# Keep-warm products of an opening on TensorE: from one f32 product each to sets of single-pass products on full rows and on row halves (mLSTM scan and gated feed-forward, one Trainium2 core)

## The chip, the cores and the metric

One Trainium2 chip (trn2), one core. The metric is the device time of one execution in microseconds (us). Three runs of the kernel before took 532.8, 534.25 and 534.55 us; the median is 534.25.

## The reference, cut to what matters

Four batches, eight heads, 768 steps, heads of 40. Per step and head a 40x40 state is faded, gets an outer product, and is read by the query; then a feed-forward with two gates follows on all 3072 rows of 320.

```
m_new = max(f_gate + m, i_gate)
C = exp(f_gate + m - m_new) * C + exp(i_gate - m_new) * outer(v, k)
n = exp(f_gate + m - m_new) * n + exp(i_gate - m_new) * k
y = sigmoid(o_gate) * (C @ q) / max(|n . q|, 1)
x = y as rows of 320
out = (sigmoid(x @ w_gate) * (x @ w_val)) @ w_out
```

## The kernel before

The 768 steps are six chunks of 128, so there are 24 units (chunk, batch). Within a chunk the scan is done with matrices: transposes of q and k (tile `pt`), scores (`s`) against a decay matrix `d`, a product with v (`av`), an outer product that carries the state on (`cs`), and a transpose of the finished rows (`xt`) into the feed-forward's input. That input is split into a high part `xh` (copied by ScalarE, `dx`, L789) and a low part `xl` (VectorE, `dy`, L796). The weights are read as pairs of words, decoded on ScalarE and VectorE (tile `dc`, from the staging tiles `st`, `st2`, `st_o`) and split into high and low parts in the same way. The feed-forward up (`pg`, L865) and down (`po`, L903) then run as single-pass products of such parts, three where one f32 product would be.

The order of all work is written out by hand: every step puts a function under a short key, and the string ORDER names the keys in the order in which they are issued; each engine runs its instructions in that order. Buffers and their waits come from tile pools by tag; a tag with one buffer makes its next user wait for the last reader or writer of the one before.

The change lies in `opening()` (L928). `warm` is an f32 tile of zeros, 128x256, set by VectorE (key `iw`, L931). `warming()` (key `im`) multiplies it six times while the first inputs arrive. `keep_warm(n)` (L967, key `iq`, twelve of them) is one f32 product of 128x128 with 128 columns on `warm`, into the PSUM tag `pg1`; nothing reads it. An f32 product is shown by the trace as two records. In ORDER the twelve `iq` stand where TensorE waits for the two first units: `iq` 0 behind the last score of unit 1, `iq` 1 behind the product with v of unit 1, `iq` 2 to 5 behind `cs` of unit 1 and ahead of the transpose `d1` (its tile is `xt_1`), `iq` 6 and 7 behind `d1`, then the first `pg` product of the feed-forward (`t0`), then `iq` 8 to 11, then the rest of `t0`.

The tiles that these steps meet: the tag `pg1` is also the second half of the first feed-forward pair; the tag `po1` holds a score of unit 1 and later a feed-forward result; the tag `gl` holds the low part of the gated values, two buffers, first used by VectorE about 33 us into the span.

Of the kernel before, what the change touches and what calls it, by code (L numbers as in the profile page):

```python
# [9 lines left out]
F32 = mybir.dt.float32  # L10
F32R = mybir.dt.float32r
# [223 lines left out]
def mlstm_then_gated_ffn_kernel(  # L235
# [13 lines left out]
    nc = tc.nc  # L249
    B, H, S, D = q.shape  # L250
    P = 128
    L = P
# [18 lines left out]
    two = ctx.enter_context(tc.tile_pool(name="two", bufs=2))  # L271
    dram = ctx.enter_context(tc.tile_pool(name="dram", bufs=1, space=bass.MemoryType.DRAM))
    ps_o = ctx.enter_context(tc.tile_pool(name="ps_o", bufs=1, space=bass.MemoryType.PSUM))
# [27 lines left out]
    def put(key, f, *args):  # L301
        todo.setdefault(key, []).append((f, args))
# [543 lines left out]
    gh, gl, po = {}, {}, {}  # L846
# [81 lines left out]
    def opening():  # L928
        us = ((0, 0), (0, 1))
        warm = two.tile([P, 2 * P], F32, tag="gh", name="warm")  # L930
        put("iw", nc.vector.memset, warm, 0.0)  # L931
        put("if", nc.sync.dma_start, fg, f_gate.rearrange("b h s -> (b h) s"))
        put("ii", nc.scalar.dma_start, ig, i_gate.rearrange("b h s -> (b h) s"))
        put("ie", nc.scalar.activation, warm[:1, P : P + 1], warm[:1, P : P + 1], AF.Exp)
# [31 lines left out]

        def keep_warm(n):  # L967
            pw = ps_o.tile([P, NT], F32, tag="pg1", name=f"pkeep{n}x")
            nc.tensor.matmul(pw[:, :P], warm[:, :P], warm[:, :P], start=True, stop=True)

        for n in range(PARAM["keep"]):
            put("iq", keep_warm, n)
# [92 lines left out]
    for c in range(NCH):  # L1065
        kc = PARAM["K"][c]
        tiles += [(c, j, 0, 2) for j in range(kc)] + [(c, j, 2, 4) for j in range(kc)]
        tiles += [(c, j, 0, 4) for j in range(kc, NF)]
    NU = NCH * B
    opening()  # L1070
    for n in range(len(tiles)):
        ffn_up(n)
# [25 lines left out]
    with tc.manual_schedule():  # L1098
        for word in ORDER.split():
# [3 lines left out]
            key, _, n = word.partition("*")  # L1103
            for _ in range(int(n or 1)):
                f, args = todo[key].pop(0)
# [30 lines left out]
```

## Time and profile before

| | |
|---|---|
| median of three runs | 534.25 us (532.8 to 534.55) |
| span of the profiled execution (its own time from the first to the last instruction) | 530.6 us |
| what the median has over that span | 3.65 us |
| TensorE busy | 518.2 us, 98% of the span, 4763 records |
| VectorE, ScalarE, GpSimd busy | 313.5, 218.8, 148.5 us |
| granted TensorE clock | 1.00 in all 40 slices |

A time in the trace counts from the span's start. Busy time of TensorE is the union of its products' records; a record's length holds the way through the array too, so products that follow closely overlap in it, and what one costs its successor is read from start to start. The share of 98% is a mean over the span: the stretch that the change touches, 16 to 25 us, and the one behind it, up to 50 us, are read apart. "Idle before <-releaser" is the time that an engine sat idle ahead of an instruction, and what ended it.

### The profile page before, as it was taken

How to read it: one execution, taken by the hardware profiler on the slowest of the kernel's cores; microseconds unless marked ns; L12 is line 12 of the kernel's file. 1: busy time of each engine (PE TensorE's matmuls, PEld its weight loads, DVE VectorE, ACT ScalarE, POOL GpSimd, SP SyncE). 2: the span in 40 equal slices, each digit the busy share in tenths (PEclk: the TensorE clock that was granted, in tenths of full speed). 3: DMA queues.
4: the chain of work that ended last, by engine and by line, in shares of the span. 5: the costliest groups of instructions: out<-in, count | busy, mean ns of one | idle time of the engine just before them, and what ended most of it. 6: DMA issues, size and time to landing. Idle time of an engine off the chain costs nothing.

```text
span 530.6 us, 12275 instructions
## 1 busy us (share of the span) xinstructions
PE 518.2 (98%) x4763; PEld 466.9 (88%) x4763; DVE 313.5 (59%) x783; ACT 218.8 (41%) x585; POOL 148.5 (28%) x219
## 2 busy tenths in 40 slices
PE   8969999999999999999999999999999999999997
PEld 6657988888999999998888888888888888999997
DVE  6999989887566557445645525646644553533323
ACT  6597676643524541443333443251333432212221
POOL 6544223455322312413124140334201101111110
PEclk9999999999999999999999999999999999999999
DMA  9998885423767965587388377578386364000000
GB/s 209 241 265 228 217 188 148 134 41 80 187 145 190 176 161 107 126 190 157 102 188 177 104 201 177 115 175 170 93 179 157 90 138 102 26 13 14 26 2 25
DMA packets 131649, 72.42 MB, mean 136 GB/s; under 512 B 103112, under 2 KB 120776, under 8 KB 131592
## 3 DMA queue, kind: packets, MB, share of 16 engines
q1 hardware_dynamic: 130504, 71.39, 56.9%
q8 instruction: 37, 0.61, 0.5%
q10 hardware_dynamic: 1088, 0.26, 0.3%
q14 instruction: 20, 0.16, 0.1%
HBM read 56.95 MB, written 14.68 MB: 135 GB/s over the span
## 4 chain that ended last, share of the span: by engine, by line
PE 88%; DVE 3%; DMA 3%; ACT 3%; issue 1%; POOL 1%; SPq 0%; DVEq 0%; ACTq 0%; POOLq 0%
PE pg L865 50%; PE po L903 23%; PE av L663 3%; PE pt L572 2%; PE s L693 2%; PE in L714 2%; PE cs L818 2%; DMA st_o<-in_moe_w_out_dram 2%; PE xt L783 1%; PE s L688 1%; ACT d L420 1%; DMA k<-in_k_dram 1%; DMA mscr<-m 1%; ACT dc L465 0%; ACT qk L587 0%
## 5 line engine op out<-in xcount | busy, mean ns | idle before, releaser
L878 ACT ACTIVATE sg<-pg 128x256 f32<-128x256 f32 (+1 forms) x103 | 48.4, 469 | 185.1 <-PE pg L865 174.9
L865 PE MATMUL pg<-xh,wh 128*128 128x256 f32 (+1 forms) x412 | 111.0, 337 | 2.6 <-ACT sg L878 2.5
L881 DVE SCALAR_TENSOR_TENSOR sg<-sg,pg 128x256 f32<-128x256 f32 (+1 forms) x103 | 54.1, 525 | 99.0 <-ACT sg L878 80.2
L865 PE MATMUL pg<-xl,wh 128*128 128x256 f32 (+1 forms) x412 | 109.7, 333 | 0.0
L865 PE MATMUL pg<-xh,wl 128*128 128x256 f32 (+1 forms) x412 | 108.9, 331 | 0.0
L892 POOL TENSOR_TENSOR gl<-sg,gh 128x256 fp32r<-128x256 f32 (+1 forms) x45 | 44.5, 988 | 186.0 <-ACT gh L886 107.1
L903 PE MATMUL po<-ol,gh 128*128 128x320 f32 x288 | 91.8, 321 | 0.0
L903 PE MATMUL po<-oh,gh 128*128 128x320 f32 x288 | 90.1, 318 | 0.9 <-ACT gh L886 0.9
L903 PE MATMUL po<-oh,gl 128*128 128x320 f32 x288 | 89.8, 318 | 0.0
L865 PEld LDWEIGHTS pg<-xh,wh 128*128 128x128 f32 x412 | 70.0, 188 | 8.6 <-ACT sg L878 4.0
L865 PEld LDWEIGHTS pg<-xl,wh 128*128 128x128 f32 x412 | 69.3, 188 | 5.3
L865 PEld LDWEIGHTS pg<-xh,wl 128*128 128x128 f32 x412 | 69.7, 188 | 4.6
L865 PE MATMUL pg<-xl,w 128*128 128x256 f32 (+1 forms) x206 | 59.3, 332 | 0.0
L903 PEld LDWEIGHTS po<-oh,gh 128*128 128x128 f32 x288 | 53.9, 188 | 4.3 <-ACT gh L886 1.4
L903 PEld LDWEIGHTS po<-oh,gl 128*128 128x128 f32 x288 | 54.0, 189 | 2.9 <-DVE gl L892 0.2
L903 PEld LDWEIGHTS po<-ol,gh 128*128 128x128 f32 x288 | 54.2, 189 | 2.2
L865 PE MATMUL pg<-xh,w 128*128 128x256 f32 (+1 forms) x206 | 53.5, 330 | 0.0
L699 DVE TENSOR_TENSOR d<-s,d 128x384 f32<-128x384 f32 (+1 forms) x66 | 33.2, 509 | 25.4 <-PE s L693 22.9
L420 ACT ACTIVATE d<-d,at 128x128 f32<-128x128 f32 x136 | 42.9, 392 | 2.8 <-DMA d<-mscr 2.8
L886 ACT ACTIVATE gh<-sg 128x256 fp32r<-128x256 f32 (+1 forms) x61 | 31.2, 512 | 28.7 <-DVE sg L881 24.5
L441 POOL TENSOR_SCALAR_AFFINE_SELECT d<-d 128x1024 f32<-128x1024 f32 x22 | 25.4, 1153 | 46.2 <-ACT d L420 28.4
L865 PEld LDWEIGHTS pg<-xl,w 128*128 128x128 f32 x206 | 36.1, 189 | 2.1
(168 smaller groups left out, 758.7 us busy)
## 6 DMA issues: line engine op xcount, KB each, us to landing
d<-mscr SPq DMA_DIRECT2D x22, 512.0 KB
ks<-scr SPq DMA_DIRECT2D x16, 360.0 KB
qs<-scr SPq DMA_DIRECT2D x16, 360.0 KB
k<-in_k_dram SPq DMA_DIRECT2D x24, 160.0 KB
v<-in_v_dram SPq DMA_DIRECT2D x24, 160.0 KB
o<-in_o_gate_dram SPq DMA_DIRECT2D x24, 160.0 KB
st_o<-in_moe_w_out_dram SPq DMA_DIRECT2D x12, 320.0 KB
out_dram<-ob SPq DMA_DIRECT2D x24, 160.0 KB
```

The costliest lines, as they stand in the source:

```text
L420: nc.scalar.activation(d[:, h, :], d[:, h, :], AF.Exp, bias=at[:, c, b * H + h : b * H + h + 1], scale=-1.0)
L441: nc.gpsimd.affine_select(out=d, in_=d, pattern=[[0, H], [1, L]], compare_op=ALU.is_ge, fill=0.0, base=0, channel_multiplier=-1)
L572: nc.tensor.transpose(pt[g][:r, x, :], t[u][:, h0 : h0 + nh, :].rearrange("p h d -> p (h d)"), ident)
L663: nc.tensor.matmul(dst[xs], lhs[:, xs], rhs, start=True, stop=True)
L693: nc.tensor.matmul(ps[g][:, m, :], ks[: 3 * D, 3 * m + g, :], qs[: 3 * D, 3 * m + g, :], start=True, stop=True)
L699: nc.vector.tensor_tensor(x, ps[g][:, :nh, :], x, ALU.mult)
L865: nc.tensor.matmul(pg[x], w[:, a, fs] if a < 2 else w[:, fs], y[c][:, a, n0:n1], start=first, stop=a == 2 and y is xl)
L878: nc.scalar.activation(sg[0], pg[0], AF.Tanh, scale=0.5)
L881: nc.vector.scalar_tensor_tensor(sg[0], sg[0], 1.0, pg[1], ALU.add, ALU.mult)
L886: nc.scalar.activation(gh[u][:, :nt], sg[0], AF.Copy)
L892: E('gl0' if c == 0 else 'gl', f'tl{n}').tensor_tensor(gl[u][:, :nt], sg[0], gh[u][:, :nt].bitcast(F32), ALU.subtract)
L903: nc.tensor.matmul(po[t], g[c, j, t0][:, (t - t0) * P : (t - t0 + 1) * P], o[:, j, :], start=j == 0 and first, stop=j == NF - 1 and last)
```

## The change

The twelve keep-warm steps stay where they are in ORDER, and the first set (`warming`) stays as it is. VectorE copies `warm` once into `zeros`, a tile of the single-pass type in the tag `gl`. Each `keep_warm(n)` becomes one of four sets of products with 256 columns on `zeros`, by n modulo 4: 0 is four pairs of half products (rows 0 to 63 into the tag `pg1`, rows 64 to 127 into the tag `po1`, in turn), 1 is four products on full rows, 2 is three times a full product and a pair of halves, 3 is four halves of the one kind and then four of the other. That is 8, 4, 9 and 8 products, three times each: 87 in place of 12.

```diff
         warm = two.tile([P, 2 * P], F32, tag="gh", name="warm")
-        put("iw", nc.vector.memset, warm, 0.0)
+        zeros = two.tile([P, 2 * P], F32R, tag="gl", name="zeros")
+
+        def blank():
+            nc.vector.memset(warm, 0.0)
+            nc.vector.tensor_copy(zeros, warm)
+
+        put("iw", blank)
...
         def keep_warm(n):
             pw = ps_o.tile([P, NT], F32, tag="pg1", name=f"pkeep{n}x")
-            nc.tensor.matmul(pw[:, :P], warm[:, :P], warm[:, :P], start=True, stop=True)
+            form = n % 4
+            pws = (pw, pw) if form == 1 else (pw, ps_o.tile([P, 4 * L], F32, tag="po1", name=f"pkeep{n}y"))
+            half = (slice(0, 64), slice(64, P))
+
+            def halves(y):
+                nc.tensor.matmul(pws[y][:, : 2 * P], zeros[half[y], :P], zeros[half[y]], start=True, stop=True)
+
+            def full():
+                nc.tensor.matmul(pws[0][:, : 2 * P], zeros[:, :P], zeros, start=True, stop=True)
+
+            if form == 0:
+                for x in range(4):
+                    halves(0)
+                    halves(1)
+            elif form == 1:
+                for x in range(4):
+                    full()
+            elif form == 2:
+                for x in range(3):
+                    full()
+                    halves(0)
+                    halves(1)
+            else:
+                for y in range(2):
+                    for x in range(4):
+                        halves(y)
```

On TensorE, between `cs` of unit 1 and the transpose of unit 1 (`xt_1`), the kernel before has the steps 2 to 5 as four products, each waiting for the one before it:

```order
L818 MATMUL cs_1_402<-v_1_234,k_1_136 80x82
L969 MATMUL pkeep2x<-warm 128x128 [waits PE_49]
L969 MATMUL pkeep3x<-warm 128x128 [waits PE_49]
L969 MATMUL pkeep4x<-warm 128x128 [waits PE_49]
L969 MATMUL pkeep5x<-warm 128x128 [waits PE_49]
L783 MATMUL xt_1_438<-ident,x_1_409 128x128 [waits DVE_49]
```

In the changed kernel 29 products stand there; from the ninth, the end of step 2, on (L980 is a half product, L983 a full one, x writes the tag `pg1` and y the tag `po1`):

```order
L980 MATMUL pkeep2y<-zeros 128x256
L980 MATMUL pkeep3x<-zeros 128x256 [waits PE_49]
L980 MATMUL pkeep3x<-zeros 128x256 x3
L980 MATMUL pkeep3y<-zeros 128x256 [waits PE_49]
L980 MATMUL pkeep3y<-zeros 128x256 x3
L980 MATMUL pkeep4x<-zeros 128x256 [waits PE_49]
L980 MATMUL pkeep4y<-zeros 128x256 [waits PE_49]
...
L983 MATMUL pkeep5x<-zeros 128x256 [waits PE_49]
L983 MATMUL pkeep5x<-zeros 128x256 x3
L783 MATMUL xt_1_479<-ident,x_1_422 128x128 [waits DVE_49]
```

The transpose stands behind 29 products in place of 4, with a wait of TensorE for itself at the start of each tile, x and y apart.

The same on TensorE between the first and the second product of the feed-forward (`pg_0_0_0`), steps 8 to 11, before:

```order
L865 MATMUL pg_0_0_0_472<-xh_407,wh_98 128x256 [waits Activation_49]
L969 MATMUL pkeep8x<-warm 128x128 [waits PE_49]
L969 MATMUL pkeep9x<-warm 128x128 [waits PE_49]
L969 MATMUL pkeep10x<-warm 128x128 [waits PE_49]
L969 MATMUL pkeep11x<-warm 128x128 [waits PE_49]
L865 MATMUL pg_0_0_0_472<-xh_407,wh_98 128x256
```

And in the changed kernel, its beginning and its end:

```order
L865 MATMUL pg_0_0_0_530<-xh_420,wh_98 128x256 [waits Activation_49]
L980 MATMUL pkeep8x<-zeros 128x256 [waits PE_49]
L980 MATMUL pkeep8y<-zeros 128x256 [waits PE_49]
...
L980 MATMUL pkeep11x<-zeros 128x256 [waits PE_49]
L980 MATMUL pkeep11x<-zeros 128x256 x3
L980 MATMUL pkeep11y<-zeros 128x256 [waits PE_49]
L980 MATMUL pkeep11y<-zeros 128x256 x3
L865 MATMUL pg_0_0_0_530<-xh_420,wh_98 128x256
```

Nothing else changes its place on any engine. VectorE has one row more, the copy into `zeros`, second in its queue.

## Rows read from the trace of the kernel before

**Rows 1.** The page, part 1: busy time of the engine, share of the span, records.
```profile
PE 518.2 (98%) x4763; PEld 466.9 (88%) x4763; DVE 313.5 (59%) x783; ACT 218.8 (41%) x585; POOL 148.5 (28%) x219
```

**Rows 2.** By stretch: busy us (records) of PE, PEld, DVE, ACT, POOL; PEclk; DMA share; GB/s.
```profile
25.00:30.00 5.00, 3.33 (x26) 2.89 (x25) 4.93 (x17) 4.57 (x15) 0.66 (x1) 1.00 1.05 281
30.00:35.00 5.00, 3.75 (x24) 2.68 (x22) 4.96 (x11) 5.00 (x19) 3.24 (x4) 1.00 0.79 223
35.00:40.00 5.00, 3.72 (x21) 2.75 (x22) 4.54 (x12) 4.23 (x13) 2.60 (x3) 1.00 1.00 279
40.00:50.00 10.00, 8.92 (x173) 7.04 (x172) 9.54 (x29) 7.77 (x23) 5.30 (x8) 1.00 0.80 200
...
60.00:120.00 60.00, 60.00 (x451) 50.97 (x449) 52.96 (x121) 36.96 (x94) 21.87 (x31) 1.00 0.56 136
```

**Rows 3.** The chain that ended last, 20 to 50 us: start us, us, what.
```profile
20.93 5.65 DMA st_o<-in_moe_w_out_dram
...
34.75 3.93 DMA st_o<-in_moe_w_out_dram
...
49.53 0.80 PE cs L818 x6
```

**Rows 4.** TensorE in order of time: start us, us, what, count, idle before.
```profile
16.27 0.39 PE L969 MATMUL pkeep0x<-warm 128*128 128x128 f32 x2
16.59 0.82 PE L663 MATMUL av<-v,d 128*32 128x41 f32 x64
17.33 0.49 PE L969 MATMUL pkeep1x<-warm 128*128 128x128 f32 x2
18.14 0.63 PE L783 MATMUL xt<-ident,x 128*128 128x128 f32 x3 [0.32 <-POOL x L761]
...
19.17 0.42 PE L969 MATMUL pkeep2x<-warm 128*128 128x128 f32 x2
19.65 0.49 PE L969 MATMUL pkeep3x<-warm 128*128 128x128 f32 x2
20.20 0.49 PE L969 MATMUL pkeep4x<-warm 128*128 128x128 f32 x2
...
21.23 0.55 PE L783 MATMUL xt<-ident,x 128*128 128x128 f32 x3
21.62 0.39 PE L969 MATMUL pkeep6x<-warm 128*128 128x128 f32 x2
...
22.36 0.38 PE L865 MATMUL pg<-xh,wh 128*128 128x256 f32 x1
...
24.49 0.37 PE L865 MATMUL pg<-xh,wh 128*128 128x256 f32 x1
...
25.63 0.64 PE L865 MATMUL pg<-xh,wl 128*128 128x256 f32 x4
...
26.35 0.28 PE L865 MATMUL pg<-xl,w 128*128 128x256 f32 x1
...
28.11 0.50 PE L865 MATMUL pg<-xh,wh 128*128 128x256 f32 x2 [1.31 <-ACT sg L878]
```

**Rows 5.** TensorE, the last products with v of unit 1, stretch 17.2 to 17.4.
```profile
17.00 0.40 PE L663 MATMUL av<-v,d 128*32 128x41 f32 x22
```

**Rows 6.** ScalarE in order of time.
```profile
21.82 0.49 ACT L789 ACTIVATE xh<-xt 128x384 fp32r<-128x384 f32 x1
...
27.69 0.37 ACT L878 ACTIVATE sg<-pg 128x256 f32<-128x256 f32 x1
...
36.38 0.44 ACT L465 ACTIVATE dc<-st 128x256 f32<-128x256 f32 x1 [0.37 <-DMA st<-in_moe_w_val_dram]
...
38.70 0.49 ACT L465 ACTIVATE dc<-st_o 128x320 f32<-128x320 f32 x1 [0.40 <-DMA st_o<-in_moe_w_out_dram]
```

**Rows 7.** VectorE in order of time.
```profile
0.93 0.27 DVE L1106 MEMSET warm<- 128x256 f32 x1 [0.93 <-PEq L1121]
3.31 0.41 DVE L1106 TENSOR_TENSOR_SCAN gin<-bmask,gin 32x128 f32<-32x128 f32 x1 [2.11 <-POOL ident masks.py:197]
```

## The prediction

> **What bounds the kernel now.** I read the busy time first, then the same by stretch, then the chain that ended last, then the order of time on TensorE and ScalarE. TensorE is busy 98% of the span [rows 1], but that is a mean. By stretch it idles between 25 and 50 us: 1.67, 1.25, 1.28 and 1.08 us are missing in the four stretches, 5.28 together, and from 60 to 120 us it has 60.00 of 60.00 [rows 2]. The chain agrees: at 20.93 us it runs through a weight transfer (`st_o`, 5.65 us to landing), then through ScalarE to a second one at 34.75 us, and only from 49.53 us on does it stay on TensorE [rows 3]. So TensorE is not what ends last in the opening, though its queue stands close behind; whatever lag it has when the stretch at 50 us begins stays to the end, since nothing idles there to take it up. The granted clock is 1.00 in every stretch read [rows 2], so the keep-warm products have no slow stretch left to repair, and I see nothing the change could win.
>
> **Prices.** Three are needed, all start to start, since records of neighbours overlap.
>
> A single-pass product with 256 columns: four of `pg` at 25.63 take 0.64 us, the last being about 0.28 long as the one at 26.35 [rows 4]; (0.64 - 0.28) / 3 = 0.12 us.
>
> A restart, where a new tile of a tag waits for the last product of the one before: the keep-warm tiles at 19.65 and 20.20 are 0.55 apart [rows 4]. Each holds one f32 product, two records of 128 columns and two passes each, as long in streaming as 256 single-pass columns, so about 0.11 each; 0.55 - 0.22 = 0.33 us per restart.
>
> A switch between full rows and halves, and whether two halves overlap, no row shows, since no product of this kernel lies on half the rows. The nearest rows are the products with v, which take a quarter of the columns: 64 records in 0.82 us [rows 4], 0.013 us each, while 41 columns in two passes at the price above need 0.12 x 82 / 256 = 0.04. So products on different quarters do overlap, and I take it that two halves of the rows do too: a pair costs 0.12, not 0.24. The other end is that they don't overlap. For the switch, the last record with v begins near 17.20 (17.00 + 0.40 less its length of some 0.2) [rows 5], and the full product behind it at 17.33 [rows 4]: about 0.12 us with next to nothing streamed between. I take 0.12 per switch; the ends are 0, if changing rows costs nothing, and 0.33, if it is a whole restart.
>
> **The change, step by step.** *The copy into `zeros`.* A copy of 128x256 on VectorE, about as long as the memset of that size, 0.27 us, stands ahead of an instruction that waits 2.11 us for GpSimd [rows 7]: nothing, and without that cover 0.27. The first set waits for the memset alone. The tag `gl` is used again by VectorE near 33 us, behind all keep-warm products: nothing.
>
> *Steps 0 and 1.* Four pairs in place of one f32 product: 0.48 for 0.21, and a switch. The products with v begin about 0.3 to 0.4 later than 16.59, step 1 near 17.7, and its four products end near 18.2. The transpose behind it waited for GpSimd until 18.14 [rows 4]. So it starts 0.1 late. The new wait of `pkeep0y` for VectorE's reading of the score is over by then. If the halves don't overlap, 0.5 more.
>
> *Steps 2 to 5.* With overlapping halves the four forms cost 6, 8, 4 and 4 prices of 0.12 (form 3 has four equal halves in a row, twice, so nothing to overlap with): 22 x 0.12 = 2.64. Three restarts (the y tile of step 4 waits for step 3, which ended just ahead of it) make 0.99, six switches inside form 2 make 0.72; the other switches fall into a restart. That is 4.35 us where 19.17 to 21.23 [rows 4] are 2.06: +2.29. The transpose `xt_1` starts near 23.6.
>
> *Steps 6 and 7.* They start 0.39 behind `xt_1` (21.23 to 21.62). Forms 2 and 3: 14 x 0.12 + 0.33 + 0.72 = 2.73, where before it was 22.36 - 21.62 = 0.74 [rows 4]: +1.99. The first `pg` also waits for ScalarE's `xh`, which ended 1.08 after `xt_1` began (21.23 to 21.82 + 0.49) [rows 4, 6], so near 24.7; the queue, at 26.8, is now the later of the two.
>
> *Steps 8 to 11.* The `pg` product 0.12, 2.64 of streaming, four restarts 1.32 (`pkeep8y` waits for `pkeep7y`), switches 0.72: 4.80 for 24.49 - 22.36 = 2.13 [rows 4]: +2.67.
>
> So the second `pg` product starts 0.1 + 2.29 + 1.99 + 2.67 = **7.05 us late**, near 31.5.
>
> **What of it is covered.** Before, the first pair's products end at 26.35 + 0.28 = 26.63 [rows 4], and ScalarE takes them (`sg`) at 27.69 [rows 6], being late itself: 1.06 of slack. Behind `sg`, ScalarE's queue is full (5.00 of 5.00 us from 30 to 35 [rows 2]) and TensorE waits for it again, 1.31 us at 28.11 [rows 4]; held by order, both move together by what is left, 5.99. VectorE follows, for it waits for `sg` and the products too. Further on ScalarE waits twice for transfers, 0.37 and 0.40 us [rows 6]; those have more time now and should be there: 0.77 less. What is late next, the `sg` at 43 us, is ScalarE's own queue. So 7.05 - 1.06 - 0.77 = **+5.2 us** at 50 us, and at the end. The profiled span would go from 530.6 to 535.8; the median of the runs is 534.25, 3.65 above that span, and so 539.4.
>
> By the row a change of shape costs 0.12 us. The Trainium skill, TensorEngine Tiling (Array Packing), Key Properties, says that a change of the tiling mode, not of the tile alone, drains the engine, which speaks against this change; by it, with a drain as dear as a restart, the time is that of the dear switches below, 543.2, by the row 539.4. For the overlap of halves no run here shows what the Trainium skill, TensorE: Matmul & The Clock Gate, Part 3 (The mechanism), states, that products on different row groups run at once.
>
> **The rivals.** *Cheap switches.* If rows are changed for nothing, 18 x 0.12 = 2.16 falls away: 7.05 - 2.16 = 4.9 late, +3.1 after the cover, 537.3 us. For it speaks that the halves lie on other rows, not on another split of the columns as the products with v; against it the 0.12 of the row.
>
> *Halves in a row, one after the other.* Seven prices more in each set of four steps, three in steps 6 and 7, 0.5 at step 0: 14 x 0.12 + 0.36 + 0.5 = 2.5. With free switches 4.9 + 2.5 = 7.4, +5.6, 539.8 us, next to my number; with 0.12 each 9.6 late, +7.7, 542.0. The overlap of the products with v speaks against it.
>
> *Dear switches.* If TensorE must run empty at each change between full rows and halves, each costs a restart: 18 x 0.33 = 5.94 in place of 2.16, so 10.8 late, +9.0, 543.2 us. For it speaks that a restart is the price of running empty [rows 4], against it the 0.12 behind the products with v [rows 5].
>
> *Absorbed, not slower.* The opening is paced by transfers, not by order: while ScalarE waits for the first pair, the transfers run on, and behind it ScalarE catches up until TensorE's 5.28 us of idle time are all used. With free switches, 4.9 - 5.28 is below zero, no change, 534.2 us; any gain beyond it has no place in the rows. It decides as soon as the lag at 26 us is under about 5 and ScalarE, once it has `sg`, is faster than before. For it: two landings on the chain [rows 3], 9.6 us. Against it: only 0.77 us of ScalarE's waits are for those landings behind 28 us [rows 6], and its queue is full.
>
> **How the numbers follow.** A measurement of this kernel tells about 0.3%, 1.6 us, from no change. My forecast with its neighbour (7 to 8 late, +4.2 to +6.5): 0.50. Cheap switches (+1.7 to +4.2): 0.22. Dear ones (0.06), or halves in a row with a switch of 0.12 (0.07), over +6.5 to +9.0: 0.13. Absorbed: 0.15, of which 0.12 within 1.6 us and 0.03 faster. So faster 0.03, same 0.12, slower 0.85. The range goes from 536.0 (most of the cheap case in, the absorbed one out) to 542.0, the two-fold dear one; some 0.2 lie outside.
>
> **What would show it.** TensorE has 63 records more, 4826 if none is missing. The halves of forms 0 and 2 start nearly together, and the next pair 0.12 later. `xt_1` starts near 23.6, the two `pg` products near 26.8 and 31.5, `sg` near 33.7 with some 5 to 6 us of idle time on ScalarE ahead of it; TensorE's 1.31 us wait at 28.11 shrinks to some 0.3; behind 50 us the records repeat, shifted by one amount, at clock 1.00. I am wrong in the price if the two `pg` products come elsewhere, in the overlap if the halves start 0.12 apart, and in the cover if they come as said and the shift at 50 us is below 3 us or above 6.5.

## The result, and the profile after

The changed kernel took 538.55 us in the median of three runs (537.64 to 538.89), against 534.25: the ratio is 1.0084, with an interval of 1.0057 to 1.0111, so it is slower, by 4.3 us. The forecast was 539.4, +5.2. A second measurement, in another set of runs (e9 below), gave 536.88 against 532.83, ratio 1.0067 (1.0051 to 1.0083).

The profiled execution of the change has a span of 536.8 us and took 538.55, so 1.75 lie around the span. The busy line and the head of the chain on its page, to be held against [rows 1] and [rows 3]:

```profile
PE 526.7 (98%) x4826; PEld 473.8 (88%) x4826; DVE 314.0 (58%) x784; ACT 218.9 (41%) x585; POOL 148.2 (28%) x219
...
PE 92%; DVE 3%; ACT 1%; issue 1%; POOL 1%; DMA 1%; SPq 0%; DVEq 0%; ACTq 0%; POOLq 0%
```

The 63 further records are there (4763 to 4826), and TensorE's share of the chain went from 88% on the page of before to 92%: the opening has joined it. By stretch, to be held against [rows 2] (busy us of PE, PEld, DVE, ACT, POOL, then clock, DMA share, GB/s):

```profile
25.00:30.00 5.00, 4.89 (x37) 3.46 (x36) 3.61 (x12) 2.68 (x9) 0.00 (x0) 1.00 0.98 247
30.00:35.00 5.00, 4.88 (x35) 3.69 (x34) 3.00 (x10) 0.85 (x2) 0.00 (x0) 1.00 0.90 267
35.00:40.00 5.00, 3.45 (x27) 2.93 (x26) 3.65 (x7) 4.94 (x17) 3.26 (x3) 1.00 0.96 259
40.00:50.00 10.00, 8.80 (x110) 6.61 (x110) 9.61 (x27) 9.72 (x31) 4.30 (x5) 1.00 0.53 129
...
60.00:120.00 60.00, 60.00 (x467) 51.84 (x467) 54.84 (x130) 38.45 (x96) 19.57 (x27) 1.00 0.64 157
```

Before, ScalarE was full from 30 to 35 us and TensorE idled; now TensorE is busy 4.88 us of five there and ScalarE works 0.85. ScalarE, which used to hold TensorE up, is waiting behind the keep-warm sets. From 60 to 120 us TensorE is busy 60.00 of 60.00 us in both.

TensorE in order of time in the changed kernel, to be held against [rows 4]:

```profile
16.07 0.82 PE L663 MATMUL av<-v,d 128*32 128x41 f32 x64
...
21.75 0.39 PE L983 MATMUL pkeep2x<-zeros 128*128 128x256 f32 x1
22.06 0.38 PE L980 MATMUL pkeep2x<-zeros 64*128 64x256 f32 x1
22.07 0.38 PE L980 MATMUL pkeep2y<-zeros 64*128 64x256 f32 x1
22.38 0.39 PE L983 MATMUL pkeep2x<-zeros 128*128 128x256 f32 x1
22.70 0.38 PE L980 MATMUL pkeep2x<-zeros 64*128 64x256 f32 x1
22.70 0.38 PE L980 MATMUL pkeep2y<-zeros 64*128 64x256 f32 x1
23.14 0.38 PE L980 MATMUL pkeep3x<-zeros 64*128 64x256 f32 x1
23.17 0.38 PE L980 MATMUL pkeep3y<-zeros 64*128 64x256 f32 x1
23.36 0.28 PE L980 MATMUL pkeep3x<-zeros 64*128 64x256 f32 x1
23.39 0.28 PE L980 MATMUL pkeep3y<-zeros 64*128 64x256 f32 x1
...
25.31 0.49 PE L783 MATMUL xt<-ident,x 128*128 128x128 f32 x3
25.55 0.36 PE L983 MATMUL pkeep6x<-zeros 128*128 128x256 f32 x1
...
28.23 0.38 PE L865 MATMUL pg<-xh,wh 128*128 128x256 f32 x1
...
32.87 0.39 PE L865 MATMUL pg<-xh,wh 128*128 128x256 f32 x1
...
35.49 0.51 PE L865 MATMUL pg<-xh,wh 128*128 128x256 f32 x2 [0.30 <-ACT sg L878]
```

The second `pg` product starts at 32.87 instead of 24.49, 8.38 us late. But 1.81 of that is there before the first changed product: the first products with v start at 16.07 here and at 14.26 in the kernel before, behind the same TensorE instructions. The loads of the weights of `mb`, in the middle of that stretch, tell why (kernel before, then the change; shortest, median and longest in ns):

```profile
L990 PEld LDWEIGHTS mb<-m,ident x32: 186/190/192, 6.1 to 9.7; 128*128 128x128 f32 x32
```
```profile
L1021 PEld LDWEIGHTS mb<-m,ident x32: 190/310/337, 6.5 to 12.2; 128*128 128x128 f32 x32
```

In the profiled execution of before, TensorE had its full rate by then; in that of the change the rows run at half the rate until past 10 us, though the page's clock reads 1.00 for both. Run e9, the same change, was late too; e3 and e5 below, whose TensorE instructions up to there are the same, were early (14.54 and 14.73 us to the first product with v), and e2, e4, e6 and e7, also the same up to there, late (15.58 to 16.24). So it is the execution that differs, not the kernel. So the sets themselves cost 8.38 - 1.81 = **6.57 us** of lag, measured from the first product with v: 32.87 - 16.07 = 16.80, before 24.49 - 14.26 = 10.23.

ScalarE, to be held against [rows 6]:

```profile
33.75 0.38 ACT L587 ACTIVATE qk<-pt 120x256 f32<-120x256 f32 x1 [2.82 <-PE pt L572]
35.06 0.38 ACT L878 ACTIVATE sg<-pg 128x256 f32<-128x256 f32 x1 [0.93 <-PE pg L865]
...
43.26 0.45 ACT L465 ACTIVATE dc<-st 128x256 f32<-128x256 f32 x1
...
45.09 0.48 ACT L465 ACTIVATE dc<-st_o 128x320 f32<-128x320 f32 x1
```

ScalarE now waits for TensorE ahead of the first pair, and the two transfers that it waited for, 0.37 and 0.40 us, are there when it comes.

### The profile page after: what moved, and what is told of

The parts are those of the page before. It is cut to its first block, busy times and chain, and to the rows that moved or that the text cites. A ratio compares the mean times of both kernels' runs of the same rounds, so it can differ in the third digit from the quotient of the medians.

```text
span 536.8 us, 12401 instructions
## 1 busy us (share of the span) xinstructions
PE 526.7 (98%) x4826; PEld 473.8 (88%) x4826; DVE 314.0 (58%) x784; ACT 218.9 (41%) x585; POOL 148.2 (28%) x219
## 4 chain that ended last, share of the span: by engine, by line
PE 92%; DVE 3%; ACT 1%; issue 1%; POOL 1%; DMA 1%; SPq 0%; DVEq 0%; ACTq 0%; POOLq 0%
PE pg L865 50%; PE po L903 23%; PE av L663 3%; PE pt L572 3%; PE in L714 2%; PE s L693 2%; PE cs L818 2%; PE xt L783 1%; PE s L688 1%; PE mb L1021 1%; DMA k<-in_k_dram 1%; PE s L1062 0%; PE pt L1039 0%; DVE d L699 0%; ACT sg L878 0%
```

## The experiments

Times are against the kernel before on the same chip in the same set of runs (533.01, 533.04 and 532.83 us in the three sets). "Lag" is the start of the second `pg` product less that of the first product with v, less the 10.23 us of before; it leaves out what the opening's rate does ahead of it.

**e1, the copy alone.** The twelve steps are those of before; `zeros` is made and not used.

```diff
-            form = n % 4
...
+            nc.tensor.matmul(pw[:, :P], warm[:, :P], warm[:, :P], start=True, stop=True)
```

> The change's copy into zeros stays, with its buffer in the tag gl; the twelve keep-warm steps are the f32 products of before. Queue theory (the whole cost is the length of TensorE's queue between the last score of unit 1 and the first feed-forward pair): no difference to the kernel before, 534.3 us, and the second pg product follows the first keep-warm product by 8.2 us as before (24.49 - 16.27). Rival, the cost comes with the copy (0.29 us on VectorE ahead of the gates) or with the buffer: 535 us or more, with the delay visible on VectorE before 6 us. Rival, the copy shifts when TensorE's opening reaches its full rate: the weight loads of 128 columns stay at 333 ns up to 10 us, as in the changed kernel's profile, and the time is 1 to 2 us above before.

532.27 us, ratio 0.997 (0.9949 to 0.9991), lag -0.1. The copy and its buffer cost nothing; that it should be faster by a quarter of a per cent has no place in its trace, and five runs against the spread of before (531.99 to 534.93) don't make me believe it. Its opening was a late one, 15.36 us to the first product with v against 14.62 in e11, the kernel before with an early one, and both have a span of 530.0 us: in the kernel before a late opening can hide.

**e2, full products alone.**

```diff
-            form = n % 4
+            form = 1
```

> All twelve steps become the set of four full-row products: no halves, no switch between shapes, 48 products instead of 87. Queue theory with the prices of the changed kernel's trace (0.12 per product, 0.32 per restart, so 0.80 per step where before it was 0.55): the second pg product comes 2.8 us later than before against the first keep-warm product, less 1.0 at the first sg and up to 0.85 more by 50 us: +1.0 to +1.7, 535.3 to 536.0 us. Rival, any larger set costs the same since the restarts carry it: +4.3 as the change, 538.5 us.

533.44 us, ratio 0.9998 (0.9985 to 1.0011): no difference, less than I expected. The lag is 2.46 (said: 2.8). Two of its rows:

```profile
25.98 0.74 PE L983 MATMUL pkeep8x<-zeros 128*128 128x256 f32 x4
26.77 0.74 PE L983 MATMUL pkeep9x<-zeros 128*128 128x256 f32 x4
```

0.79 us per set, as priced. So of 2.5 us of lag on TensorE at most 0.6 show in the time, by the interval.

**e3, pairs alone.**

```diff
-            form = n % 4
+            form = 0
```

> All twelve steps become the set of four pairs of halves, 96 products. If two halves run at once as in the changed kernel's trace (starts 4 ns apart, pairs 0.12 apart), a step costs the same 0.80 us as four full products and the time is that of the run with full products alone, 535.3 to 536.0 us, although it has twice the products. Rival, products are paid one by one: 0.48 more per step, 5.8 us over twelve steps, 541 us.

534.82 us, ratio 1.0021 (1.0007 to 1.0036), +1.8; lag 3.46. A set of eight halves (the first rows of steps 2 and 3):

```profile
19.78 0.38 PE L980 MATMUL pkeep2x<-zeros 64*128 64x256 f32 x1
19.78 0.38 PE L980 MATMUL pkeep2y<-zeros 64*128 64x256 f32 x1
20.00 0.28 PE L980 MATMUL pkeep2x<-zeros 64*128 64x256 f32 x1
20.01 0.28 PE L980 MATMUL pkeep2y<-zeros 64*128 64x256 f32 x1
...
20.57 0.38 PE L980 MATMUL pkeep3x<-zeros 64*128 64x256 f32 x1
```

The set takes 0.79 us too, so twice the products at the same price, far from the rival's 541. The 1 us by which the lag exceeds that of e2 I did not expect; the sets are equal, and the two traces put it at the ends of the blocks, where halves give way to products on all rows or the other way round: from the last set to the `pg` behind it 0.70 us in place of 0.57, from `xt_1` to step 6 0.48 in place of 0.25.

**e4, the mixed set in another order.**

```diff
                 for x in range(3):
                     full()
+                for x in range(3):
                     halves(0)
                     halves(1)
```

> The change, with the set that mixes shapes put in another order: three full products first and then the three pairs, so one switch inside it where there were five; the same products. Switch price 0.20 us from the changed kernel's trace: 3 sets x 4 switches x 0.20 = 2.4 us less lag, 538.55 - 2.4 = 536.2 us. Rival, the mixed set is dear for its nine products and not for the switches: no difference to the change, 538.5 us.

535.46 us, +2.45, ratio 1.0036 (1.0020 to 1.0052); lag 4.19, 2.4 less than the change's 6.57, as the switches were priced. Step 2, whose nine products took 21.14 to 23.14 in the change:

```profile
20.78 0.60 PE L983 MATMUL pkeep2x<-zeros 128*128 128x256 f32 x3
21.31 0.38 PE L980 MATMUL pkeep2x<-zeros 64*128 64x256 f32 x1
...
21.99 0.38 PE L980 MATMUL pkeep3x<-zeros 64*128 64x256 f32 x1
```

1.21 us for the same nine products, 0.8 less. The mixed set is dear for its order, not for its work.

**e5, all halves on the same rows.**

```diff
-            half = (slice(0, 64), slice(64, P))
+            half = (slice(0, 64), slice(0, 64))
```

> The change with every half product on rows 0 to 63: as many products, the same PSUM tiles and switches, but none on the other half of the rows. Theory, the halves of the change run at once because they lie on different rows: here they are paid one by one, 4 x 0.12 more per set of pairs, as much per set of four and four, 3 x 0.12 more per mixed set, three of each: 3.96 us more lag, so 8.2 us above before where the change had 4.3. Rival, the overlap has to do with the two PSUM tiles and not with the rows: the time of the change.

543.61 us in the median of four, 539.8 to 548.35, ratio 1.0169 (1.0105 to 1.0232). The pairs no longer start together:

```profile
16.82 0.38 PE L980 MATMUL pkeep0x<-zeros 64*128 64x256 f32 x1
17.05 0.28 PE L980 MATMUL pkeep0y<-zeros 64*128 64x256 f32 x1
17.17 0.27 PE L980 MATMUL pkeep0x<-zeros 64*128 64x256 f32 x1
17.28 0.28 PE L980 MATMUL pkeep0y<-zeros 64*128 64x256 f32 x1
```

0.12 apart, in turn, though on two PSUM tiles as before: it is the rows that let them run at once. The two executions with a mean granted clock of 0.999 took 539.8 and 540.65, 6.8 and 7.6 above before, near the 8.2 expected. The other two (mean clock 0.987 and 0.981) lost more. The profile is of one of them, and shows another reason:

```profile
15.00:25.00 10.00, 10.00 (x174) 7.90 (x161) 7.43 (x20) 4.06 (x10) 6.67 (x8) 0.99 0.92 232
25.00:35.00 10.00, 10.00 (x37) 8.07 (x36) 6.61 (x20) 3.15 (x10) 0.00 (x0) 0.50 0.95 246
35.00:45.00 10.00, 9.94 (x36) 7.91 (x35) 0.00 (x0) 0.49 (x2) 0.00 (x0) 0.50 0.55 147
45.00:55.00 10.00, 7.81 (x47) 5.93 (x47) 8.78 (x20) 10.00 (x34) 6.49 (x6) 0.98 0.14 41
```

The granted clock is 0.50 for some 20 us, 1.2 GHz, while TensorE is busy all the time; ahead of that, from 20 us on, it ran half products one after the other with full ones among them.

**e6 and e7, the sets in some steps alone**, the other steps as before.

```diff
+            if n > 5:
+                nc.tensor.matmul(pw[:, :P], warm[:, :P], warm[:, :P], start=True, stop=True)
+                return
             form = n % 4
```

(in e7 `n < 8`)

> The sets of the change in steps 0 to 5 alone, steps 6 to 11 as before. From the traces, xt_1 then starts 2.25 us later against the first product with v (9.23 for 6.98) and nothing behind it adds, so the first pair is 2.25 late; ScalarE's first sg takes up 1.1 and the stretch up to 50 us another 0.9, as the four kernels of the first set show (lag of the first sg against before 1.36, 2.46, 3.17 and 5.55 us, time 0.4, 1.8, 2.5 and 4.3 us). So +0.2 us, no difference to be measured. Rival, every microsecond of lag is paid: 4.3 x 2.25 / 6.56 = +1.5 us.

> The sets of the change in steps 8 to 11 alone, steps 0 to 7 as before. Between the two first pg products there are then 4.64 us instead of 2.13, 2.5 us of lag; less 1.1 at the first sg and 0.9 up to 50 us: +0.5 us. Rival, every microsecond is paid: +1.6 us. With the run before it: if the cover is shared, the two together add 0.7 us while the whole change adds 4.3; if it is not, they add 3.1.

e6: 533.65 us, ratio 1.0009 (0.9988 to 1.0030), lag 2.06. e7: 534.01 us, 1.0009 (0.9999 to 1.0019), lag 2.37. By the ratios that is about +0.5 us each, +1.0 together, with an uncertainty of some 1.2 for the sum of the two. At the price that the whole change pays, 4.3 us for 6.57 of lag, the two lags together, 4.43, would make 2.9, and that is outside; e6 by itself would not exclude it. The cover is shared: each part alone hides under it, all together don't.

**e8, no keep-warm products.**

```diff
-            nc.tensor.matmul(pw[:, :P], warm[:, :P], warm[:, :P], start=True, stop=True)
+            pass
```

> The kernel before without any of the twelve keep-warm products. Theory, the queue is not what ends last there before the change: the second pg product comes up to 1.9 us earlier and the first sg at the same time, since it stands behind ScalarE's own work and a transfer; 0 to -0.5 us, if the clock stays at 1.00. Rival, the products hold the clock: without them records at half the rate show somewhere between 16 and 30 us (weight loads of 128 columns 333 ns and not 188), and the time is 1 to 4 us longer.

532.72 us, ratio 0.9991 (0.9981 to 1.0000). The time came as the theory had it. The slow records came as the rival had them, without its price:

```profile
20.00:25.00 5.00, 2.59 (x10) 2.12 (x11) 4.93 (x10) 3.10 (x10) 2.89 (x3) 0.67 1.03 245
25.00:30.00 5.00, 4.25 (x20) 3.86 (x19) 4.90 (x18) 3.85 (x12) 0.34 (x1) 0.50 0.90 254
30.00:35.00 5.00, 4.29 (x26) 3.74 (x26) 4.83 (x12) 4.78 (x16) 1.51 (x3) 0.80 0.88 255
```

The granted clock falls to 0.50 near 21.7 us, at the end of a stretch in which TensorE idled 2.13 us ahead of `xt_1`, and comes back near 32 us. The first `sg` is at 28.01, against 27.69 with the products [rows 6]; counted from the first product with v that is 13.40 against 13.43. So the products of before do hold the clock, and at this place it is worth nothing, since TensorE isn't what ends last there.

**e9, the change again; e10 and e11, nine products in the first set, in the change and in the kernel before; e12, nine products there and none later.**

```diff
-    'warm': 6,
+    'warm': 9,
```

> The change itself once more, as the anchor beside the runs of before on this chip: 4.3 us above before. In its trace the lag of the second pg product against the first product with v should be 6.56 us again, whatever the rate of TensorE's records before 11 us; a lag that follows that rate would mean that the sets are not what costs.

> The change, with nine f32 products in the first set and not six: they end near 5.1 us, about when k has landed, so the 0.7 to 1.1 us in which TensorE stood idle there are filled. Of ten traces so far four show the full rate (weight loads of 128 columns 190 ns and not 333) from 4.1 to 4.7 us on and six from 8.9 to 10.9 us only, and in these the first product with v starts 1.1 to 1.9 us later. If the idle gap is what keeps the rate down, the full rate comes by 8.5 us in every execution; the change has no slack left behind the opening, so 0.5 to 1 us less than the change beside it. Rival, the gap has nothing to do with it: rates as before, and no difference.

> The same nine products in the kernel before. Full rate by 8.5 us as in the run ahead, but here the first sg has 1.1 us of slack against TensorE, so 0 to -0.5 us against before. Rival, the opening's rate is paid in full: -1 us.

> No keep-warm products behind the first set, and nine products in the first set: the run without them was 0.1% below before although TensorE's granted clock fell to 1.2 GHz for 10.2 us from 21.7 us on. If that stretch lies under ScalarE's work, the earlier full rate adds what it adds to before: -0.3 to -0.8 us against before, the fastest of all. Rival, a slow stretch that begins at another time reaches products that are not covered: executions 1 to 2 us above the others.

e9: 536.88 us, +4.05, lag 6.51, with the opening at half rate until past 10 us again. e10: 536.91 us, lag 6.38, with the full rate early: the lag is the sets' own, at either rate. The time is no better than that of e9, against what I expected. The trace of e10 shows the wait for `k` gone and the full rate from 5.5 us on (here, the first transposes of `q` and `k`):

```profile
5.26 0.41 PE L1039 MATMUL pt<-ident,q 128*80 128x128 f32 x1
5.47 0.31 PE L1039 MATMUL pt<-ident,k 128*80 128x128 f32 x1
```

and a span of 534.8 against 536.6 in e9; but the profile of e9 (538.35 us) is the slowest of its five runs, and the four others (536.24 to 537.17) lie where e10's do. Only the profiled execution shows when the full rate came, so this stays open for the four. e11: 533.51 us, ratio 1.0021 (1.0001 to 1.0040), not the gain I expected; its runs reach from 532.4 to 537.07, the longest at a mean clock of 0.990. e12: 532.30 us, ratio 0.9990 (0.9979 to 1.0000), within what can't be told from no change. Nothing here beats the kernel before by more than 0.1% with certainty.

The lags and the times side by side:

| kernel | lag of the second `pg`, us | time against before, us |
|---|---|---|
| e1 | -0.1 | -0.7 |
| e6 | 2.06 | +0.6 |
| e7 | 2.37 | +1.0 |
| e2 | 2.46 | +0.4 |
| e3 | 3.46 | +1.8 |
| e4 | 4.19 | +2.45 |
| e10 | 6.38 | +4.1 |
| the change (e9 in brackets) | 6.57 (6.51) | +4.3 (+4.05) |

Up to some 2 us of lag cost little; beyond that each microsecond of lag is close to one of time. With 2 us taken off, every line from e2 down is met within 0.5 us.

## Why the prediction was right

The sign, the place and the mechanism came as said: a longer queue on TensorE between `cs` and the first feed-forward pair, ScalarE waiting for it, and the rest of the kernel shifted by nearly one amount. Point by point.

*The prices.* A product or a pair of halves 0.12 us: the halves of a pair start within 0.01 of each other, and the next pair of a set follows 0.12 later. A restart 0.33: from the last pair of step 2 to step 3, 23.14 - 22.70 = 0.44, 0.12 of it streaming, so 0.32. The switch was the term that I had from the farthest rows, 0.12 with ends of 0 and 0.33: a pair behind a full product comes 22.06 - 21.75 = 0.31 later and a full product behind a pair 0.32, less 0.12 of streaming, **0.20 us**. So it is dearer than products with v made it, and cheaper than the whole restart that I read into the rule of the Trainium skill, TensorEngine Tiling (Array Packing), Key Properties, that a change of the tiling mode drains the engine. That a change of mode costs something, the trace agrees, and e4 removes twelve of them for 2.4 us.

*Form 3.* "Form 3 has four equal halves in a row, twice, so nothing to overlap with" was wrong: the second kind starts 0.03 us behind the first and the two run in parallel, 23.14, 23.17, 23.36, 23.39, four prices and not eight. That put 3 x 4 x 0.12 = 1.44 us too much into the lag. The switches put in too little: I counted six inside each mixed set, and the order full, pair, full, pair, full, pair has five, so 15 x 0.20 = 3.0 us stand against my 2.16, 0.84 short. The mistakes have opposite signs and leave 0.6 of the 1.44, close to the 0.48 by which the lag came out too long:

| stretch | said | trace of the change |
|---|---|---|
| steps 2 to 5, to `xt_1` | 4.35 | 25.31 - 21.14 = 4.17 |
| steps 6 and 7, to the first `pg` | 2.73 | 28.23 - 25.55 = 2.68 |
| first to second `pg` | 4.80 | 32.87 - 28.23 = 4.64 |
| lag in all | 7.05 | 6.57 |

That the sum came this near is in part luck. The step that was most wrong is the price of form 3, and the price and count of the switches made up for more than half of it.

*The cover.* 1.06 us at the first `sg` and 0.77 from the two transfers were said, 1.83 in all. The first part is there: 8.38 late at the second `pg`, 35.06 - 27.69 = 7.37 at the `sg`, so 1.01, and TensorE's wait of 1.31 us at 28.11 became 0.30. The second part came out by luck. Both transfers are no longer waited for; but neither are they in e11, the kernel before with a longer first set, whose first two `sg` come only 0.2 us later than in the trace that I read:

```profile
34.93 0.37 ACT L878 ACTIVATE sg<-pg 128x256 f32<-128x256 f32 x1
36.20 0.44 ACT L465 ACTIVATE dc<-st 128x256 f32<-128x256 f32 x1
38.09 0.50 ACT L465 ACTIVATE dc<-st_o 128x320 f32<-128x320 f32 x1
```

So the two waits can be absent without any such lag, and it isn't shown that the lag of the change removed them. The traces of e11 and e10, the kernel before and the change, both with the early full rate, are the fair pair. The second `pg` product is 31.23 - 24.65 = 6.58 us later in e10, the first `sg` 33.42 - 27.88 = 5.54 and the third 48.72 - 43.17 = 5.55: 1.04 is covered at the first `sg` and nothing between it and the third. The spans are 534.8 and 530.0, 4.8 apart, so another 0.7 is covered later. About half of it is a wait of TensorE for VectorE, which the trace of e11 has, that of before too (at 124.07), and those of e10 and the change have not:

```profile
123.38 0.83 PE L818 MATMUL cs<-v,k 128*120 128x123 f32 x6 [0.33 <-DVE t L718]
```

That TensorE has nothing left to give behind 50 us was thus not quite so; where the rest is saved stays open. In all the pair gives 6.58 - 4.8 = 1.8, the size that was said; the runs of the table, lag less time, give 1.7 to 2.5 from e2 down.

*The base of the sum.* I set 3.65 us between the span of the profiled execution and the median. The runs of the change show 1.75 between their own span and time. With as much, the profile of before, at a span of 530.6, is an execution of 532.35 us, faster than all three of its timed runs, and one with the early full rate; that of the change has the late one. So the spans differ by 6.2 and the medians by 4.3. Against the spans my number would have been 1 us short and against the medians it is 0.9 long; the lag, measured from where the change begins, is the figure to compare, and it was said 0.5 too long.

*The rivals.* Cheap switches are refuted by e4, halves in a row by e3 and e5 (same rows, in turn, and some 2.5 us or more longer than the change), the copy and its buffer by e1. "Absorbed" is right for lags of about 2 us (e2, e6, e7) and wrong for the change: of 6.58 us of lag some 1.8 are taken up, although TensorE had 5.28 us of idle time behind.

## What to carry to other kernels

Filler on an engine is free up to the slack of the waits behind it, and in this kernel that slack was shared by all filler ahead of it: twelve sets of 0.8 us in place of products of 0.55 cost at most 0.6 us (e2), sets of pairs and full products with three of the twelve mixed in shape 4.3, and 2.45 with those three grouped (e4). Where products on row halves have to stand among full ones, group them by shape, since here each switch cost more than the product between. Compare traces from the point where the change begins: executions with the same TensorE instructions up to there differed by 1.7 us (14.54 in e3, 16.24 in e2). And look for a short wait in a second trace before counting on it as slack: two of those that the forecast used are missing from a trace in which the engine came only 0.2 us later.

## What the runs showed that I had not expected

TensorE did not keep to the order of the program across row halves: four products on rows 0 to 63 followed by four on rows 64 to 127 started in turn, one of each kind, 0.03 us apart. The Trainium skill, TensorE: Matmul & The Clock Gate, Part 3 (The mechanism), has products start strictly in order; it is the trace that decides, and the 0.79 us which the set of eight took, as much as four full products, says the same. With all halves on rows 0 to 63, in e5, the same eight did keep to the order of the program and took 23.43 - 22.36 = 1.07 us to the next set:

```profile
22.36 0.74 PE L980 MATMUL pkeep3x<-zeros 64*128 64x256 f32 x4
22.95 0.64 PE L980 MATMUL pkeep3y<-zeros 64*128 64x256 f32 x4
```

The granted clock fell to 0.50 in the trace of e5, near 25 us, although the records show TensorE busy 10.00 of 10.00 us from 15 to 25; two other executions of e5 kept a mean of 0.999. Why isn't settled here. In e8 it fell for some 10 us without any loss of time. In the opening, behind six products of the same kind, the full rate came between 4 and 5 us in four of the first ten traces and between 9 and 11 us in six, and the first product with v came at 14.26 to 14.73 us in the four and at 15.36 to 16.24 in the six; a longer first set, with at most 0.3 us of gap behind it (e10 to e12), showed the early rate in three traces of three, and no gain in the median.
